# Left factors of w1, w2 loaded one factor at a time, two right factors in two buffers, and the next group's sums an item sooner

## The chip, the cores and the metric

One core of one Trainium2 chip runs the whole program. The metric is device time in microseconds (us), of one execution. Three executions of the kernel before took 1446.51, 1443.76 and 1447.54 us (median 1446.51). A fourth one, taken with the profiler, took 1452.29 us.

## The reference

```python
p_packed = sm_attn(p, k, v)             # 8 batches, 8 heads, 576 rows of 64, 32 packed rows
attn_out = sm_attn(q, p_packed, p_packed)
x = attn_out.transpose(0, 2, 1, 3).reshape(4608, 512)
h = x @ w_in                            # 512 x 2048
x2 = (h * (1 / (1 + exp(-h)))) @ w_out  # 2048 x 512
a, b = x2 @ w1, x2 @ w2                 # 512 x 1024 each
out = ((a * b) @ w3) @ w_out2           # 1024 x 1024, then 1024 x 512
```

All inputs and the output are float32. The kernel multiplies in a reduced form (float32r): each operand is split into a high part and the rest, and each product is made of three matmuls, high by high, rest by high, high by rest (`mm3`, lines 97 to 100; `split`, lines 82 to 91: ScalarE or VectorE makes the high part, VectorE or GpSimd subtracts it).

## The kernel before, in words

**Two stages.** The first stage makes x2, 256 items of 18 matmuls (`emit_h`, `emit_g`, `emit_x2`). Beside it run three streams of side work, paced by tables of (first item, last item, steps): stream "x" does the attention and later the weights w3 and w_out2, "y" the products of attention and w_in, and "z" (`decode_late`, line 914) decodes weights that the second stage needs. A "z" step is either one of 12 decodes that are only stored for later, or a step of one of four pairs of w1, w2 blocks; a pair takes two decodes and 11 steps that make and store seven left factors.

**The second stage** (from line 1117) makes a and b, their product, and the last product, by a Strassen-Winograd scheme: seven products of 2x2 blocks in place of eight. x2 is cut into 6 groups (g) of 768 rows. Each group has 4 items (mp), each a quarter of the inner width of a and b. An item has two halves, x = 0 for w1 and x = 1 for w2. In a half, `emit_ab` runs seven products (`product`, line 1306): a left factor of w1 or w2 (names a11, a12, a22, s1 to s4) by a right factor of x2 (b11, t1, b21, t2, t3, b22, t4, tiles `xcb` and `xct`), six matmuls of 384 columns each. ScalarE and VectorE take the results out of PSUM (tiles `p`, `u`, `y`); in the half x = 1 they also make the left factors of the last product (tiles `lfa`, `lfs`, sums in `tmp`). The last product of item i (`o_steps`, 63 matmuls of 256 columns, PSUM `ps_o`, running sums `o`) is put between the products of item i+1, with w34, the right factors made of w3 and w_out2, which `second_right_factors` makes in the first items.

**What the change touches.** Before, the left factors of a half come in one load of 1792 KB (`unit`, `load_unit`, line 1199) into one of three buffers, and a buffer is loaded again when its whole half is done. `load_x2` (line 1123) brings the x2 rows of a group into `x2r`, one buffer; it is called after item 2 of the group before. `right_sums` (line 1176) makes four sums on GpSimd (line 1151: tiles `xt`, `x2r`, `zz`, `zz`), and `right_factors` (line 1193) splits b11, t1 and the other five, from the beginning of item 3's half x = 1; `right_part` writes each into its only buffer, so that it must wait until the old group's last product with that factor is done. The table `paces["z"]` (line 1105) gives the "z" stream 27 steps over items 70 to 101, 26 over 128 to 165, and 12 decodes over 168 to 205.

**What sets the order.** The program is written in the order above, with generators that are called a step at a time (`side`, `step()` in `emit_ab`); a scheduler then places the instructions of each engine. Each engine works through its own list in order. All loads here are issued by SyncE (SP) in one queue, the stores of `out` too.

Of the kernel before, what the change touches and what calls it, by code (L numbers as in the profile page):

```python
# [9 lines left out]
F32 = mybir.dt.float32  # L10
# [13 lines left out]
def attention_swiglu_chain(  # L24
# [115 lines left out]
    wi_d = dram.tile([4, DM, 512], F32, name="wi_d")  # L140
    w12_d = dram.tile([128, KM2 // 2, 2, 2, 7, 2, 128], F32, name="w12_d")
    w34_d = [dram.tile([128, 512], F32, name=f"w34_d{i}") for i in range(KM2)]
# [765 lines left out]
    def decode_late():  # L908
# [7 lines left out]

        raws = []

        def load():

            raws.append(raw())
            with tc.issue_after(behind["mr"]):
                DMA.dma_start(out=raws[-1], in_=late_srcs[len(raws) - 1])

        load()
        yield
        zs = []
        for n in range(MID):
            if n + 1 < MID:
                load()  # L930
            with hold("sg"):
                z = Decode(raws[n], room(n)).z
            if n >= KM2:
# [5 lines left out]
            if n % 2:  # L939
                x, kt = divmod(n // 2, 2)  # L940
                sums = at.tile([128, 4, 256], F32, tag="wi", name="sums", bufs=WI)

                def part(j, src):
                    t = at.tile([128, 2, 2, 128], F32R, tag="z", name="w12s", bufs=NZ)
                    split(t[:, :, 0], t[:, :, 1], src.rearrange("p (j n) -> p j n", j=2), eng=G if j % 2 else V)
                    store(out=w12_d[:, 2:4, x, kt, j], in_=t, age=1)
# [39 lines left out]
    def prepare_second():  # L986

        attn.close()
        with tc.tile_pool(name="dec2", bufs=1, side="right") as dp:
# [16 lines left out]
            def combine(n):  # L1006
# [4 lines left out]
                def part(j, src):  # L1011
                    t = dp.tile([128, 2, 2, 128], F32R, tag="w12s", name="w12s", bufs=4)
                    split(t[:, :, 0], t[:, :, 1], src.rearrange("p (j n) -> p j n", j=2))
                    store(out=w12_d[:, 0:2, x, kt, j], in_=t, age=0)

# [88 lines left out]
    over(at0 + 2, at0 + 17, [Spread(B - 1, 0), Spread(B - 1, 1)])  # L1104
    paces["z"] += [(70, 101, 27), (128, 165, 26), (168, at0 + 13, MID - KM2)]
    prep_end = at0 + 2 * H2 - 6
# [12 lines left out]
    assert NG * GT == NT  # L1119
    x2r, x2c, w34 = {}, {}, {}  # L1120
    LEFT = {name: j for j, name in enumerate(("a11", "a12", "a22", "s1", "s2", "s3", "s4"))}

# [22 lines left out]
    def right_part(g, name, src, eng=None):  # L1145
        c = early.tile([128, 2, 2, W], F32R, tag=f"xc{name}", name=f"xc{name}")
        split(c[:, :, 0], c[:, :, 1], src, eng=eng)
        x2c[g][name] = c
# [30 lines left out]
    def right_sums(g):  # L1179
# [11 lines left out]
        yield  # L1191

    def right_factors(g):

        x2c[g] = {}
        for n, name in enumerate(RIGHT):
            right_part(g, name, sums_of[g][name], V if n % 2 else G)
            yield

    wunits, came2 = [], []  # L1200

    def load_unit():

        n = len(came2)
        mp, x = divmod(n % (2 * MP), 2)
        t = wunits[n % len(wunits)]
        behind["unit"] = move(out=t, in_=w12_d[:, mp, x]).ins
        came2.append(t)

    def room_unit(pool):  # L1210
        wunits.append(pool.tile([128, 2, 7, 2, 128], F32R, name=f"unit{len(wunits)}"))

# [40 lines left out]
    for i, (b, f, m) in enumerate(items):  # L1253
# [14 lines left out]
        if i == prep_end:  # L1268
# [4 lines left out]
            load_x2(0)  # L1273
            for _ in range(2):
                room_unit(early)
                load_unit()
            for mp in range(2):
                load_z34(mp)
            drain(first_right_factors())
# [18 lines left out]

    side = [second_right_factors()]
    next(side[0])  # L1300
    top = ctx.enter_context(tc.tile_pool(name="top", bufs=1))
    room_unit(top)
    load_unit()

    items2 = [(g, mp) for g in range(NG) for mp in range(MP)]

    def product(bank, w, g, left, right, first, last):

        xt = x2c[g][right]
        for kt in range(2):  # L1310
            for n, (wp, xp) in enumerate(((0, 0), (1, 0), (0, 1))):
                T.matmul(  # L1312
                    out=bank, lhsT=w[:, kt, LEFT[left], wp], rhs=xt[:, kt, xp],
                    start=first and (kt, n) == (0, 0), stop=last and (kt, n) == (1, 2),
                    skip_group_check=True,
                )

    ORDER = ("a11", "a22", "s1", "s2", "a12", "s4", "s3")
    lefts = {}

    def emit_ab(i):
# [18 lines left out]
        for x in range(2):  # L1340
            wt = came2[2 * i + x]
            nxt = side[0]
# [62 lines left out]
            step()  # L1405
            while len(came2) < min(2 * len(items2), 2 * i + x + 1 + len(wunits)):
                load_unit()
        while waiting:
# [140 lines left out]
```

## Time and profile before

| | |
|---|---|
| median of three runs | 1446.51 us (1443.76 to 1447.54) |
| profiled execution | 1452.29 us; span from first to last instruction 1450.2 us |
| TensorE (PE) busy | 1378.3 us, 95% of the span, 9188 matmuls |
| VectorE (DVE), GpSimd (POOL), ScalarE (ACT) busy | 1014.1, 900.2, 735.6 us |
| mean granted TensorE clock | 0.986 of full |

PE is the engine that sets the end: it is busy in nearly every stretch. A time can fall by PE's idle time, and by the stretches in which its clock is granted at half. The span runs from 0 to 1450 us; the second stage begins at about 870 us. Where a row says `[3.15 <-DVE y L1330]`, the engine was idle for 3.15 us before that instruction, and a VectorE instruction of line 1330 that writes tile y ended the wait.

### The profile page before, as it was taken

The numbers are of one execution on the slowest core, as the hardware profiler recorded it, in microseconds if no ns is written. First come the engines' busy times: TensorE is split into PE (matmuls) and PEld (weight loads), VectorE is DVE, ScalarE is ACT, GpSimd is POOL, SyncE is SP. The second block draws the span as 40 slices with busy tenths as digits, with TensorE's granted clock in tenths as the row PEclk, the third lists the DMA queues.
The fourth block names the chain that finished last, engine by engine and source line by source line (L and its number), as shares of the span: only waits on it lengthen the run. The fifth ranks groups of instructions, "written<-read, shape, count | busy, mean of one in ns | idle before, by whom it ended". The sixth has DMA issues, their size and how long they took to land.

```text
span 1450.2 us, 25891 instructions
## 1 busy us (share of the span) xinstructions
PE 1378.3 (95%) x9188; PEld 1322.4 (91%) x9188; DVE 1014.1 (70%) x1768; ACT 735.6 (51%) x1643; POOL 900.2 (62%) x854
## 2 busy tenths in 40 slices
PE   7799899999999999999999999999999899999998
PEld 5488799989999999999999998999999899899897
DVE  5897856568964589877678848685584756656756
ACT  6866556555665555665556645343334333333332
POOL 2768855756867666798677635374473644744733
PEclk9999999999999999999999999999999999999999
DMA  8598545745655445676647565455546545465541
GB/s 315 191 307 254 162 148 158 213 144 172 215 167 151 139 147 151 193 234 203 191 139 250 186 226 200 152 196 196 201 162 226 196 159 196 146 222 221 186 163 44
DMA packets 149922, 272.75 MB, mean 188 GB/s; under 512 B 14113, under 2 KB 107553, under 8 KB 143649
## 3 DMA queue, kind: packets, MB, share of 16 engines
q1 hardware_dynamic: 131680, 251.18, 52.5%
q10 hardware_dynamic: 18112, 19.93, 3.9%
q8 instruction: 72, 1.18, 0.3%
q14 instruction: 58, 0.47, 0.1%
HBM read 208.93 MB, written 62.13 MB: 187 GB/s over the span
## 4 chain that ended last, share of the span: by engine, by line
PE 65%; DVE 16%; ACT 5%; DMA 5%; issue 4%; POOL 2%; SPq 2%; POOLq 0%; ACTq 0%; DVEq 0%
PE ps_a L1312 11%; PE ps_o L1444 10%; PE ps_x L100 6%; PE ps_x L99 6%; PE ps_x L98 6%; PE ps_e L1312 6%; PE ps_h L98 3%; PE ps_h L100 3%; PE ps_h L99 3%; PE ps_b L1312 3%; DVE y L1330 2%; SPq L115 1%; DVE gg L846 1%; DMA mr<-m_d 1%; DMA x2r<-x_d 1%
## 5 line engine op out<-in xcount | busy, mean ns | idle before, releaser
L98 PE MATMUL ps_x<-gh,wo 128*128 128x288 f32 x1024 | 301.1, 297 | 2.0 <-ACT gh L82 1.2
L99 PE MATMUL ps_x<-gh,wo 128*128 128x288 f32 x1024 | 300.4, 296 | 0.0
L100 PE MATMUL ps_x<-gl,wo 128*128 128x288 f32 x1024 | 290.7, 297 | 3.3 <-POOL gl L91 3.2
L91 POOL TENSOR_TENSOR gl<-gg,gh 128x288 fp32r<-128x288 f32 x256 | 231.7, 908 | 98.7 <-ACT gh L82 79.9
L1426 DVE TENSOR_TENSOR o<-o,ps_o 128x768 f32<-128x768 f32 x144 | 136.3, 949 | 105.8 <-PE ps_o L1444 85.3
L91 POOL TENSOR_TENSOR mq<-mr,mq 128x256 fp32r<-128x256 f32 x168 | 140.4, 836 | 96.2 <-DVE mq L86 51.8
L98 PEld LDWEIGHTS ps_x<-gh,wo 128*128 128x128 f32 x1024 | 192.5, 188 | 4.9 <-ACT gh L82 1.4
L846 DVE SCALAR_TENSOR_TENSOR gg<-sg,ps_h 128x288 f32<-128x288 f32 x256 | 114.3, 447 | 116.1 <-ACT sg L841 59.3
L99 PEld LDWEIGHTS ps_x<-gh,wo 128*128 128x128 f32 x1024 | 192.7, 188 | 2.0 <-issue 1.2
L100 PEld LDWEIGHTS ps_x<-gl,wo 128*128 128x128 f32 x1024 | 188.4, 189 | 6.7 <-POOL gl L91 5.9
L82 ACT ACTIVATE gh<-gg 128x288 fp32r<-128x288 f32 x256 | 112.8, 443 | 155.8 <-DVE gg L846 147.8
L1312 PE MATMUL ps_a<-xct,unit 128*128 128x384 f32 x864 | 180.1, 342 | 6.2 <-DVE y L1330 5.5
L98 PE MATMUL ps_h<-a,mq 128*128 128x288 f32 x512 | 156.2, 305 | 19.2 <-DVE gg L846 14.9
L1312 PEld LDWEIGHTS ps_a<-xct,unit 128*128 128x128 f32 x864 | 150.8, 191 | 8.5 <-DVE y L1330 6.4
L99 PE MATMUL ps_h<-a,mq 128*128 128x288 f32 x512 | 152.5, 298 | 0.0
L100 PE MATMUL ps_h<-a,mq 128*128 128x288 f32 x512 | 152.1, 297 | 0.1
L841 ACT ACTIVATE sg<-ps_h 128x288 f32<-128x288 f32 x256 | 102.9, 404 | 64.7 <-PE ps_h L100 46.3
L91 POOL TENSOR_TENSOR lfa<-y,lfa 128x384 fp32r<-128x384 f32 x69 | 74.4, 1079 | 83.3 <-ACT lfa L82 83.1
L1444 PE MATMUL ps_o<-w,lfs 128*128 128x256 f32 x828 | 121.4, 283 | 4.2 <-DVE lfs L91 3.6
L98 PEld LDWEIGHTS ps_h<-a,mq 128*128 128x128 f32 x512 | 96.9, 189 | 28.5 <-DVE gg L846 21.4
L1444 PEld LDWEIGHTS ps_o<-w,lfs 128*128 128x128 f32 x828 | 113.6, 190 | 5.4 <-DVE lfs L91 4.4
L91 POOL TENSOR_TENSOR lfs<-tmp,lfs 128x384 fp32r<-128x384 f32 x69 | 78.4, 1144 | 39.7 <-ACT lfs L82 38.6
(198 smaller groups left out, 3211.7 us busy)
## 6 DMA issues: line engine op xcount, KB each, us to landing
unit<-w_d SPq DMA_DIRECT2D x48, 1792.0 KB, 6.9
mr<-m_d SPq DMA_DIRECT2D x144, 128.0 KB, 2.5
raw<-in_moe_w_dram SPq DMA_DIRECT2D x32, 512.0 KB, 4.4
w_d<-w12s ACTq DMA_DIRECT2D x56, 256.0 KB, 2.8
wz<-wi_d SPq DMA_DIRECT2D x48, 256.0 KB, 3.8
m_d<-ms SPq DMA_DIRECT2D x96, 128.0 KB, 3.0
x_d<-xs SPq DMA_DIRECT2D x20, 576.0 KB, 3.6
raw<-in_moe_w_out_dram SPq DMA_DIRECT2D x22, 512.0 KB, 4.4
```

What stands on the lines that cost most here:

```text
L82: A.activation(out=dst, in_=src, func=ACTF.Copy, scale=mul)
L91: (eng or V).tensor_tensor(out=lo, in0=src, in1=hi.bitcast(F32), op=ALU.subtract)
L98: T.matmul(out=dst, lhsT=wh, rhs=xh, start=start, stop=False)
L99: T.matmul(out=dst, lhsT=wl, rhs=xh, start=False, stop=False)
L100: return T.matmul(out=dst, lhsT=wh, rhs=xl, start=False, stop=stop)
L115: return eng.dma_start(out=out, in_=in_)
L841: ins = A.activation(out=sg, in_=ps, func=ACTF.Tanh, scale=0.5)
L846: ins = V.scalar_tensor_tensor(out=gg, in0=sg, scalar=1.0, in1=ps, op0=ALU.add, op1=ALU.mult)
L1312: T.matmul(out=bank, lhsT=w[:, kt, LEFT[left], wp], rhs=xt[:, kt, xp], start=first and (kt, n) == (0, 0), stop=last and (kt, n) == (1, 2), ...
L1330: eng.tensor_tensor(out=out, in0=in0, in1=in1, op=kind)
L1426: V.tensor_tensor(out=oacc[k], in0=oacc[k], in1=ps, op=ALU.add)
L1444: T.matmul(out=ps[:, t], lhsT=l[:, lp], rhs=w[:, wp], start=fresh and t != 1 and n == 0, stop=done and t != 0 and n == 2, skip_group_check ...
```

## The change

Four parts. (1) The left factors lie in DRAM by factor (`w12_d`), and each factor of a half is loaded alone (256 KB, `load_left`), into one of two buffers of its own; the load for two halves later is issued behind the factor's product. (2) b11 and t1 have a second buffer, used by the odd groups, in the room that the third unit had. (3) The next group's x2 rows are loaded after item 1 (in the first group after item 0); its sums and its b11 and t1 (now both split on GpSimd) are called from item 2 on, one in three steps; the other five are split in item 3's half x = 1 as before. In the first group `second_right_factors` is called with one step at a time where it had two in item 0, and the sums come right behind it. (4) The "z" stream has the 12 stored decodes in two lots of six between the pairs, and its table is 14 steps over items 70 to 101, 6 over 102 to 126, 26 over 128 to 165, 6 over 166 to 190, 13 over 191 to 206.

```diff
-    w12_d = dram.tile([128, KM2 // 2, 2, 2, 7, 2, 128], F32, name="w12_d")
+    w12_d = dram.tile([128, KM2 // 2, 2, 7, 2, 2, 128], F32, name="w12_d")
...
+        order_late = [0, 1, *others[:6], 2, 3, 4, 5, *others[6:], 6, 7]
...
-    paces["z"] += [(70, 101, 27), (128, 165, 26), (168, at0 + 13, MID - KM2)]
+    paces["z"] += [(70, 101, 14), (102, 126, 6), (128, 165, 26), (166, 190, 6), (191, at0 + 14, 13)]
...
+    TWICE = ("b11", "t1")
...
     def right_part(g, name, src, eng=None):
-        c = early.tile([128, 2, 2, W], F32R, tag=f"xc{name}", name=f"xc{name}")
+        pool = top[0] if g % 2 and name in TWICE else early
+        c = pool.tile([128, 2, 2, W], F32R, tag=f"xc{name}", name=f"xc{name}")
...
+    def two_right_factors(g):
+
+        x2c[g] = {}
+        for name in TWICE:
+            right_part(g, name, sums_of[g][name], G)
+            yield
+
     def right_factors(g):
 
-        x2c[g] = {}
         for n, name in enumerate(RIGHT):
-            right_part(g, name, sums_of[g][name], V if n % 2 else G)
+            if name not in TWICE:
+                right_part(g, name, sums_of[g][name], V if n % 2 else G)
             yield
 
-    def load_unit():
...
+    def group_sums(g):
+        for gen in (right_sums(g), two_right_factors(g)):
+            for _ in gen:
+                yield
+                yield
+                yield
+
+    def load_left(n, name):
+
+        if n < 2 * len(items2):
+            mp, x = divmod(n % (2 * MP), 2)
+            t = early.tile([128, 2, 2, 128], F32R, tag=f"w{name}", name=f"w{name}", bufs=2)
+            behind["unit"] = move(out=t, in_=w12_d[:, mp, x, LEFT[name]]).ins
+            came2[n, name] = t
...
+    def first_group():
+        yield from second_right_factors()
+        yield from right_sums(1)
+        yield from two_right_factors(1)
...
+        w = came2.pop((n2, left))
...
-                    out=bank, lhsT=w[:, kt, LEFT[left], wp], rhs=xt[:, kt, xp],
+                    out=bank, lhsT=w[:, kt, wp], rhs=xt[:, kt, xp],
...
+        load_left(n2 + 2, left)
...
-                for _ in range(1 if i else 2):
-                    next(nxt, None)
+                next(nxt, None)
...
-        if mp == MP - 1 and g + 1 < NG:
+        if g and mp == 2 and g + 1 < NG:
             drain(side[0])
-            side[0] = right_sums(g + 1)
+            side[0] = group_sums(g + 1)
         emit_ab(i)
-        if mp == MP - 2 and g + 1 < NG:
+        if mp == (1 if g else 0) and g + 1 < NG:
             load_x2(g + 1)
```

**POOL's list from the last item of group 2 towards group 3.** Of the kernel before (`tmp`, `lfa`, `lfs` are an item's own left factors, the rest is the next group's right side):

```order
L91 TENSOR_TENSOR lfa_14641<-y_14532,lfa_14641 128x384
L1151 TENSOR_TENSOR xt<-x2r 128x768
L91 TENSOR_TENSOR xcb_14798<-x2r,xcb_14798 128x2x384
L91 TENSOR_TENSOR xcb_14774<-x2r,xcb_14774 128x2x384
L1151 TENSOR_TENSOR x2r<-x2r 128x2x384
L1151 TENSOR_TENSOR zz<-x2r,xt 128x768
L91 TENSOR_TENSOR lfa_14795<-y_14764,lfa_14795 128x384
L91 TENSOR_TENSOR xct_14840<-x2r,xct_14840 128x2x384
L1151 TENSOR_TENSOR zz<-x2r,zz 128x768
L1330 TENSOR_TENSOR tmp<-y_14764,y_14766 128x384
```

Of the changed kernel, one item sooner, and then the beginning of what is left for the last item:

```order
L91 TENSOR_TENSOR lfs_14692<-tmp,lfs_14692 128x384
L91 TENSOR_TENSOR xcb_14941<-x2r,xcb_14941 128x2x384
L1159 TENSOR_TENSOR xt<-x2r 128x768
L1159 TENSOR_TENSOR x2r<-x2r 128x2x384
L1159 TENSOR_TENSOR zz<-x2r,xt 128x768
L91 TENSOR_TENSOR xct_14995<-xt,xct_14995 128x2x384
L91 TENSOR_TENSOR lfa_14867<-y_14836,lfa_14867 128x384
L1159 TENSOR_TENSOR zz<-x2r,zz 128x768
```

```order
L91 TENSOR_TENSOR xcb_15125<-x2r,xcb_15125 128x2x384
L91 TENSOR_TENSOR lfa_15122<-y_15091,lfa_15122 128x384
L91 TENSOR_TENSOR xct_15171<-x2r,xct_15171 128x2x384
L1351 TENSOR_TENSOR tmp<-y_15091,y_15093 128x384
```

The four sums, b11 and t1 stand a whole item ahead, with one left factor of item 2 among them; in the last item POOL has three of the next group's instructions (b21, t3, later t4).

**DVE's list in items 0 and 1**, where w34 is made (`w34sums` and `zz` are its sums, `w` its splits). Before, between two of item 0's adds that read `ps_a`:

```order
L1330 TENSOR_TENSOR y_12120<-p_12117,ps_a 128x384
L977 TENSOR_TENSOR w34sums<-zz,w34sums 128x256 x3
L91 TENSOR_TENSOR w_0_12104<-w34sums,w_0_12104 128x256 x2
L91 TENSOR_TENSOR w_1_12102<-w34sums,w_1_12102 128x256 x2
L91 TENSOR_TENSOR w_0_12104<-w34sums,w_0_12104 128x256
L1330 TENSOR_TENSOR y_12205<-p_12202,ps_a 128x384
```

And now:

```order
L1351 TENSOR_TENSOR y_12142<-p_12139,ps_a 128x384
L91 TENSOR_TENSOR w_0_12128<-w34sums,w_0_12128 128x256
L980 TENSOR_TENSOR w34sums<-zz,w34sums 128x256
L91 TENSOR_TENSOR w_1_12126<-w34sums,w_1_12126 128x256 x2
L91 TENSOR_TENSOR w_0_12128<-w34sums,w_0_12128 128x256
L91 TENSOR_TENSOR w_1_12126<-w34sums,w_1_12126 128x256
L91 TENSOR_TENSOR w_0_12128<-w34sums,w_0_12128 128x256
L1351 TENSOR_TENSOR y_12225<-p_12222,ps_a 128x384
```

Eight instructions for w34 stood between the two adds, and seven stand there now.

**SP's list around the x2 load for group 3** (with the semaphores that each waits for, the landings of earlier loads in turn among eight of them). Before:

```order
L115 DMA unit_12111<-w_d 128x3584 [waits DMAHW7_49,DMAHW3_49,PE_49]
L115 DMA unit_11869<-w_d 128x3584 [waits DMAHW5_49,PE_49]
L115 DMA x2r<-x_d_0_91 128x4x288 [waits DMAHW1_49,Activation_49,Pool_49]
L115 DMA x2r<-x_d_1_92 128x4x288 [waits DMAHW2_49]
L115 DMA x2r<-x_d_0_93 128x4x192
```

And now:

```order
L115 DMA ws_14767<-w_d 128x512 [waits DMAHW4_49,PE_49]
L115 DMA wa_14688<-w_d 128x512 [waits DMAHW5_49,PE_49]
L115 DMA x2r<-x_d_0_91 128x4x288 [waits DMAHW6_49,Pool_49]
L115 DMA x2r<-x_d_1_92 128x4x288 [waits DMAHW7_49]
L115 DMA x2r<-x_d_0_93 128x4x192 [waits DMAHW0_49]
L115 DMA ws_14788<-w_d 128x512 [waits DMAHW1_49,PE_49]
```

The x2 load has two loads of 256 KB right ahead of it in the place of two of 1792 KB; every load waits for the landing of the one eight places ahead.

**ACT's list in the first group's item 1:**

```order
L82 ACTIVATE p_12473<-ps_a 128x384
L82 ACTIVATE lfs_12321<-tmp 128x384
L82 ACTIVATE xcb_12996<-x2r 128x2x384
L82 ACTIVATE w_3_12713<-zz 128x256
L82 ACTIVATE o_12413<-ps_o 128x768
L82 ACTIVATE p_12474<-ps_e 128x384
```

The high part of group 1's b11 (`xcb_12996`) stands ahead of two instructions that take results out of PSUM for PE, and it reads x2 rows that are loaded after item 0.

## Rows read from the trace of the kernel before

**Rows 1.** The page: each engine's busy us, share of the span, instructions.
```profile
PE 1378.3 (95%) x9188; PEld 1322.4 (91%) x9188; DVE 1014.1 (70%) x1768; ACT 735.6 (51%) x1643; POOL 900.2 (62%) x854
```

**Rows 2.** By stretch: length, busy PE, PEld, DVE, ACT, POOL, clock, DMA share, GB/s.
```profile
288.00:395.00 107.00, 100.51 (x734) 97.72 (x732) 83.97 (x190) 61.17 (x154) 71.61 (x75) 0.98 0.56 171
471.00:600.00 129.00, 124.69 (x937) 122.80 (x936) 102.88 (x228) 73.18 (x183) 89.42 (x96) 1.00 0.51 153
600.00:712.00 112.00, 110.48 (x789) 106.97 (x788) 79.00 (x140) 66.15 (x148) 88.55 (x87) 1.00 0.65 203
870.00:912.00 42.00, 36.34 (x195) 34.69 (x196) 35.28 (x55) 22.89 (x58) 23.43 (x23) 0.92 0.45 175
912.00:1441.00 529.00, 511.67 (x3324) 505.77 (x3323) 341.31 (x449) 193.14 (x372) 279.94 (x223) 0.99 0.50 180
```

**Rows 3.** PE's waits in order of time, 889 to 910 us: start, length, instruction, idle before.
```profile
891.59 0.66 PE L1312 MATMUL ps_a<-xct,unit 128*128 128x384 f32 x2 [1.95 <-DVE y L1330]
909.36 1.01 PE L1312 MATMUL ps_a<-xct,unit 128*128 128x384 f32 x2 [3.15 <-DVE y L1330]
```

**Rows 4.** The same where group 1, 2, 3 and 4 begin.
```profile
969.08 0.97 PE L1312 MATMUL ps_e<-xct,unit 128*128 128x384 f32 x4 [1.74 <-DVE xct L91]
1062.49 0.85 PE L1312 MATMUL ps_e<-xct,unit 128*128 128x384 f32 x2 [1.98 <-DVE xct L91]
1158.98 1.33 PE L1312 MATMUL ps_b<-xcb,unit 128*128 128x384 f32 x3 [3.48 <-DVE y L1330]
1253.05 1.16 PE L1312 MATMUL ps_b<-xcb,unit 128*128 128x384 f32 x5 [1.13 <-DVE y L1330]
1259.80 1.41 PE L1444 MATMUL ps_o<-w,lfs 128*128 128x256 f32 x8 [2.47 <-DVE lfs L91]
```

**Rows 5.** The same where group 5 begins.
```profile
1346.46 0.74 PE L1444 MATMUL ps_o<-w,lfa 128*128 128x256 f32 x4 [1.19 <-DVE o L1426]
1352.77 1.21 PE L1444 MATMUL ps_o<-w,lfs 128*128 128x256 f32 x8 [1.12 <-DVE lfs L91]
```

**Rows 6.** PE alone by stretch: length, busy, clock; the second at full clock.
```profile
892.02:895.43 3.41, 3.41 (x13) 0.50 0.92 357
1000.00:1003.41 3.41, 3.41 (x22) 1.00 0.27 94
1062.69:1066.10 3.41, 3.41 (x12) 0.50 0.95 408
1158.26:1165.09 6.83, 6.11 (x20) 0.50 0.39 168
1260.66:1264.07 3.41, 3.41 (x14) 0.50 0.00 0
```

**Rows 7.** DVE in order of time, ahead of the wait of 3.48 us.
```profile
1154.57 1.82 DVE L1330 TENSOR_TENSOR y<-y,y 128x384 f32<-128x384 f32 x1
```

**Rows 8.** POOL in order of time at that place, and where x2 lands.
```profile
1142.06 1.85 POOL L1151 TENSOR_TENSOR xt<-x2r 128x768 f32<-128x768 f32 x1 [4.99 <-DMA x2r<-x_d]
1155.92 2.12 POOL L1151 TENSOR_TENSOR zz<-x2r,zz 128x768 f32<-128x768 f32 x1
```

**Rows 9.** DVE's instructions on tile y, 912 to 1441 us: count, ns min/median/max.
```profile
L1330 DVE TENSOR_TENSOR y<-y,y x68: 550/558/2196, 913.8 to 1431.8; 128x384 f32<-128x384 f32 x68
L1330 DVE TENSOR_TENSOR y<-p,ps_a x45: 539/554/556, 916.9 to 1431.3; 128x384 f32<-128x384 f32 x45
```

**Rows 10.** SP's waits, 870 to 1441 us: in total, times, longest.
```profile
SPq L115 <- PE ps_a L1312: 333.5, 34, 18.2
```

**Rows 11.** DMA issues, 870 to 1441 us: count, KB each, median us to landing.
```profile
unit<-w_d SPq DMA_DIRECT2D x45, 1792.0 KB, 6.8
x2r<-x_d SPq DMA_DIRECT2D x10, 576.0 KB, 9.2
zz<-w_d SPq DMA_DIRECT2D x4, 256.0 KB, 5.9
```

**Rows 12.** SP in order of time: one unit load's issue.
```profile
1130.69 0.32 SPq L115 DMA_DIRECT2D unit<-w_d  x1
```

More of the change, by code (lines that the diff above doesn't have):

```diff
@@ L917, in decode_late @@
         raws = []
+        others = list(range(KM2, MID))
+        order_late = [0, 1, *others[:6], 2, 3, 4, 5, *others[6:], 6, 7]
+        to_come = list(order_late)
         def load():
@@ L922, in load @@
             with tc.issue_after(behind["mr"]):
-                DMA.dma_start(out=raws[-1], in_=late_srcs[len(raws) - 1])
+                DMA.dma_start(out=raws[-1], in_=late_srcs[to_come.pop(0)])
         load()
@@ L927, in decode_late @@
         zs = []
-        for n in range(MID):
-            if n + 1 < MID:
+        for n in order_late:
+            if to_come:
                 load()
             with hold("sg"):
-                z = Decode(raws[n], room(n)).z
+                z = Decode(raws.pop(0), room(n)).z
             if n >= KM2:
@@ L945, in part @@
                     split(t[:, :, 0], t[:, :, 1], src.rearrange("p (j n) -> p j n", j=2), eng=G if j % 2 else V)
-                    store(out=w12_d[:, 2:4, x, kt, j], in_=t, age=1)
+                    store(out=w12_d[:, 2:4, x, j, kt], in_=t, age=1)
                 for step in left_factors(zs, sums, part):
@@ L1013, in part @@
                     split(t[:, :, 0], t[:, :, 1], src.rearrange("p (j n) -> p j n", j=2))
-                    store(out=w12_d[:, 0:2, x, kt, j], in_=t, age=0)
+                    store(out=w12_d[:, 0:2, x, j, kt], in_=t, age=0)
                 later.extend(left_factors(z, sums, part))
@@ L1120, in attention_swiglu_chain @@
     x2r, x2c, w34 = {}, {}, {}
+    USED = ("a11", "s1", "a12", "s2", "s3", "s4", "a22")
+    items2 = [(g, mp) for g in range(NG) for mp in range(MP)]
+    TWICE = ("b11", "t1")
+    top = []
     LEFT = {name: j for j, name in enumerate(("a11", "a12", "a22", "s1", "s2", "s3", "s4"))}
@@ L1191, in right_sums @@
         yield
+    def two_right_factors(g):
[3 more added lines that the diff above has]
+            yield
     def right_factors(g):
-        x2c[g] = {}
         for n, name in enumerate(RIGHT):
-            right_part(g, name, sums_of[g][name], V if n % 2 else G)
+            if name not in TWICE:
+                right_part(g, name, sums_of[g][name], V if n % 2 else G)
             yield
-    wunits, came2 = [], []
-    def load_unit():
[L1204 to L1211, printed above, removed]
+    def group_sums(g):
[4 more added lines that the diff above has]
+                yield
+    came2 = {}
+    def load_left(n, name):
[4 more added lines that the diff above has]
+            came2[n, name] = t
     z34 = {}
@@ L1273, in attention_swiglu_chain @@
             load_x2(0)
[L1274 to L1278, printed above, removed]
+            for n in range(2):
+                for name in USED:
+                    load_left(n, name)
+                load_z34(n)
             drain(first_right_factors())
@@ L1297, in room, with product @@
         return pool.tile(shape, dtype, tag=tag, name=tag)
-    side = [second_right_factors()]
-    next(side[0])
[L1301 to L1307, printed above, removed]
+    def first_group():
+        yield from second_right_factors()
+        yield from right_sums(1)
+        yield from two_right_factors(1)
+    side = [first_group()]
+    next(side[0])
+    top.append(ctx.enter_context(tc.tile_pool(name="top", bufs=1)))
+    def product(bank, n2, g, left, right, first, last):
         xt = x2c[g][right]
+        w = came2.pop((n2, left))
         for kt in range(2):
@@ L1340, in emit_ab @@
         for x in range(2):
-            wt = came2[2 * i + x]
+            wt = 2 * i + x
             nxt = side[0]
@@ L1405, in emit_ab @@
             step()
-            while len(came2) < min(2 * len(items2), 2 * i + x + 1 + len(wunits)):
-                load_unit()
         while waiting:
```

## The prediction, made before the changed kernel ran

> **What bounds the kernel now.** I read the page's busy times, then the busy times by stretch, then PE's waits in order of time, then the other engines just ahead of those waits. PE is busy 1378.3 us, 95% of the span [rows 1], so no change of order can give more than the other 5%, some 72 us, and what PE loses at half clock. The stretches show where that time lies [rows 2]. In 912 to 1441 us PE is idle for 529.00 - 511.67 = 17.3 us, in 870 to 912 for 42.00 - 36.34 = 5.7 us; that is the second stage. In the first stage, where the "z" table is changed, it is idle for 6.5 us (288 to 395), 4.3 us (471 to 600) and 1.5 us (600 to 712).
>
> In the second stage most of the idle time is a few waits. Two are in items 0 and 1, of 1.95 and 3.15 us, both ended by an add of DVE that takes a result out of PSUM [rows 3]. The others come once per group, at its beginning: 1.74 us for group 1, 1.98 for group 2, 3.48 for group 3, 1.13 and 2.47 for group 4 [rows 4], 1.19 and 1.12 for group 5 [rows 5]. The reader is to see that PE never waits for `unit`, the left factors: the waits end with DVE. Ahead of the longest one DVE spends 1.82 us on one `y<-y,y` [rows 7], whose median is 558 ns [rows 9], while POOL runs a sum of 2.12 us [rows 8]. POOL is late there because x2 landed late: it had waited 4.99 us for `x2r` [rows 8].
>
> Behind the long waits stands a second loss, the clock. Stretches of 3.41 us at half clock follow the waits of 1.95, 1.98, 3.48 (two of them, 6.83 us) and 2.47 us, and none follows 1.74 or the shorter ones [rows 3 to 6]. At half clock PE ran 13 matmuls in 3.41 us, at full clock 22 [rows 6]: a stretch costs 3.41 x 9 / 22 = 1.4 us. The mean clock of 0.92 over 42 us [rows 2] says that 870 to 912 holds two of them (8% of 42 us is 3.4 us of full clock, and each lacks half of 3.41).
>
> **The change part by part.** Sums are against the profiled execution, 1452.3 us with what lies around its span; the median of the three runs, 1446.5, is 5.8 us lower, and I subtract the same sum from it.
>
> (1) Loads by factor. 48 loads of 1792 KB become 336 of 256 KB with the same bytes. SP spends 0.32 us on an issue [rows 12], so 288 more take 288 x 0.32 = 92 us of SP in some 570 us; SP now spends 333.5 us waiting for PE to free units [rows 10], which covers it. If that cover were gone, loads would go out late, the second rival. Each factor has two buffers: its load is issued when its product is done and is needed two halves later. A half is 571 us / 48 = 11.9 us, so there are 23.8 us for it, and 256 KB landed in 5.9 us [rows 11]. Cost 0.
>
> Seven small loads for a large one is what a rule speaks against. The rows have 5.9 us to landing for 256 KB and 6.8 us for 1792 KB [rows 11], so most of it does not grow with size. The Trainium skill (DMA: Bandwidth & Descriptors, section Bandwidth) asks for transfers of 1 MiB or more, and its section on the anatomy of one DMA has a fixed 2 us in each; by its formula a factor is an estimated 2.6 us and a unit 6.1. Paid seven times in line that would be an estimated 18.2 us, over a half's length; paid side by side it changes nothing. No run here shows seven such loads under way.
>
> (2) and (3) Group begins 2 to 5. Removed from the last item: the four sums (about 2 us each on POOL, as the one of 2.12 [rows 8]), b11 and t1, and their wait for the old group's last products. POOL's list keeps three of the next group's instructions there, where it had eight. Moved to: item 2's first half, where DVE mostly reads PSUM. Its adds from PSUM take 539 to 556 ns whatever POOL does, while `y<-y,y` reaches 2196 [rows 9]; so the sums slow DVE less there. What is late next: DVE still splits t2 and b22 in the last item, ahead of the adds that free PSUM. I leave one wait of 1.2 us per begin, like the short ones of today [rows 5], and no half clock, since none followed waits of that size. Waits now 1.98 + 3.48 + 1.13 + 2.47 + 1.19 + 1.12 = 11.4 us, half clock 4 x 1.4 = 5.6 us, together 17.0; left 4.8; gain 12.2 us. Bounds: all of it, 17.0, and 0.
>
> Group 1's begin: 1.74 [rows 4] to 1.2, gain 0.5 us; bounds 1.7 and 0.
>
> Items 0 and 1. Though w34 is called at half the rate, DVE's list still has seven of its instructions between two adds where it had eight. So I take an eighth of 1.95 + 3.15, 0.6 us. The gain could be all, 5.1 + 2 x 1.4 = 7.9 us. It could be a loss: ACT now has the split of group 1's b11 in item 1, ahead of two instructions that empty PSUM for PE, and it waits there for x2 rows; POOL's 4.99 us [rows 8] is the price at that end.
>
> (4) The "z" table. In 288 to 395 us there are 27 "z" steps now and 14 then. PE's loss there is 6.5 us of waits and a half-clock stretch (mean clock 0.98 [rows 2]), 1.4 us; I take half, 4 us, as gain. The 13 steps removed turn up at 666 to 704 us, where the old table had 5 of its 12 decodes, beside the attention of the last batch; I charge 2 us, near the 1.5 that this stretch loses [rows 2]. Net 2 us, bounds 8 gain (all of it) and 6 loss (what moves costs there what it cost before, 6.5).
>
> Sum: 0 + 12.2 + 0.5 + 0.6 + 2 = 15.3 us. 1452.3 - 15.3 = 1437 for a profiled run, **1431 us** for the median.
>
> **The rivals.** *The bunch only moves (no difference).* POOL's list now has five of the next group's instructions in a row, a sixth behind one left factor of item 2, together about 12 us, and they begin only when x2 has landed. If it lands 9.2 us after its issue [rows 11], the block ends some 21 us into an item of 23.8 us, and item 2's left factors, which follow on POOL, come late for the products of item 3. For it: POOL waited 4.99 us for x2 before, and DVE's instructions with two SBUF inputs slow down wherever POOL runs [rows 7, 9]. The Trainium skill (SBUF — State Buffer, section Who interferes with whom) has it that those contend with GpSimd's reads and those with one SBUF input do not; the trace agrees, 2196 against 556 ns. Against it: the loads ahead of x2 are 256 KB now, so that it should land sooner. Price: a wait of 2 us and a half-clock stretch, 3.4 us, in five groups, 17 us: what (2) and (3) gave goes back, and 1446 to 1448 us is the time.
>
> *Loads become the bound (slower).* SP's list shows each load waiting for the landing of the one eight places ahead, so at most eight are under way. A group has 56 factor loads, 3 or 4 of x2 and 4 stores: 64 in turn on eight semaphores, 8 landings one after the other in about 95 us (group begins at 969, 1062, 1159 [rows 4]). This decides as soon as a landing takes over 95 / 8 = 11.9 us. Rows of before have 5.9, 6.8 and 9.2 us [rows 11]; against it also that the DMA engines are busy half the time, 0.50 [rows 2]. At 12.5 us a group takes 100 us: 6 x 5 = 30 us lost, 15 gained, 1461 us. The rule of the Trainium skill on small transfers, above, would do it in this way.
>
> **How the numbers follow.** The forecast with its bounds has a chance of 0.75, the moved bunch 0.16, the loads 0.09. The best end is 17.0 + 1.7 + 7.9 + 8 = 34.6 us, 1412 us. The worst end of the forecast has (2) and (3) at half, 6, a loss of 5 in items 0 and 1, and 6 in the first stage: 5 us slower than now. That all three go wrong together is unlikely, and the moved bunch ends near 1447, so the range is 1412 to 1447 us. About 0.3% (4.3 us) is what a measurement can tell from no change. Faster 0.75, within it 0.16, slower 0.09.
>
> **What would show it.** Right: group begins with waits of some 1.2 us or less and a granted clock of 1.00 there; the rows of `xt` on POOL beginning in item 2, not in the last item; PE waiting nowhere for a `w` factor's DMA; the two waits in items 0 and 1 still there. Wrong: PE waits ended by POOL `lfa` or `lfs` about an item before a group begins (the moved bunch); PE waits ended by a DMA of `wa` or `ws`, or SP rows with landings over 12 us (the loads); ACT waiting for `x2r` in item 1 with PE behind it; new waits of PE at 660 to 710 us.

## The result and the profile after

| | before | after |
|---|---|---|
| median of four runs each, us | 1447.03 (1443.76 to 1448.73) | 1425.7 (1424.89 to 1427.32) |
| profiled execution, its span, us | 1452.29, 1450.2 | 1427.32, 1425.5 |
| start of the second stage, us | 870.0 | 864.4 |

The ratio is 0.9857, interval 0.9837 to 0.9876: 20.7 us less by the ratio (the medians differ by 21.3). The forecast was 1431, range 1412 to 1447.

The page and the stretches of after, to be laid beside [rows 1, 2]; the last two begin 6 us earlier, as the second stage does, and end 9 us ahead of the span's end, as there. The page first:

```profile
PE 1368.4 (96%) x9188; PEld 1315.7 (92%) x9188; DVE 1016.3 (71%) x1763; ACT 733.5 (51%) x1643; POOL 903.0 (63%) x859
```

Then the stretches, with their columns:

```profile
288.00:395.00 107.00, 104.44 (x776) 102.71 (x776) 81.44 (x192) 61.35 (x152) 70.38 (x79) 0.98 0.55 168
600.00:712.00 112.00, 111.73 (x807) 109.42 (x807) 84.19 (x143) 67.92 (x155) 86.52 (x89) 1.00 0.61 190
864.00:906.00 42.00, 35.43 (x207) 33.41 (x208) 35.96 (x57) 23.41 (x58) 25.58 (x24) 1.00 0.76 244
906.00:1416.00 510.00, 502.26 (x3318) 499.29 (x3318) 337.38 (x445) 190.51 (x372) 283.23 (x228) 1.00 0.60 182
```

The second stage after items 0 and 1, up to 9 us ahead of the end, lost 19 us of length (529 to 510). PE's idle time there fell from 17.3 to 7.7 us, and the clock column from 0.99 to 1.00. In 864 to 906, items 0 and 1, PE is idle for 6.6 us where it was 5.7: nothing was gained there but the clock (0.92 to 1.00). 288 to 395 went from 6.5 to 2.6 us idle, and 600 to 712 from 1.5 to 0.3.

The best single measure of the group begins is the stretch from the start of group 1 to the start of group 5, which holds the same products in both kernels. Busy times by stretch, of before:

```profile
963.60:1341.70 378.10, 365.68 (x2364) 362.11 (x2363) 243.84 (x318) 140.19 (x269) 204.94 (x161) 0.98 0.52 190
```

The same of after:

```profile
957.50:1317.00 359.50, 356.65 (x2364) 355.62 (x2363) 238.17 (x314) 138.91 (x270) 209.74 (x165) 1.00 0.65 199
```

It is 18.6 us shorter. (A second trace of the old second stage, that of the version with the new "z" table alone, has 377.4 us here.) PE's idle time in it (length less busy time) is 12.4 us before and 2.9 after. Of the 9.0 us that PE is busy for less, some 5.6 are the four half-clock stretches of [rows 6] that lie in it, at the estimate of 1.4 us each; the other 3.4 us this view doesn't resolve. Group 0 is 0.5 us shorter and the last group, with the end, as long as before within 0.1 us. So of the 24.7 us of span, 5.6 come from the first stage, 0.5 from group 0 and 18.6 from groups 1 to 4. The profiled execution of before lies 5.3 us above its median, that of after 1.6 us above its own, so some 4 of the 24.7 us belong to these two executions; the part on the "z" table shows that the first stage is where such a difference can lie.

These are the waits of PE that are left in groups 0 to 5 and last over 0.9 us, ahead of the end (waits in order of time, to be laid beside [rows 3 to 5]):

```profile
883.58 1.32 PE L1332 MATMUL ps_a<-xct,wa 128*128 128x384 f32 x6 [2.42 <-DVE y L1351]
898.59 1.33 PE L1462 MATMUL ps_o<-w,lfs 128*128 128x256 f32 x9 [1.43 <-DVE lfs L91]
919.35 1.31 PE L1462 MATMUL ps_o<-w,lfs 128*128 128x256 f32 x9 [1.52 <-ACT lfs L82]
1119.59 0.62 PE L1462 MATMUL ps_o<-w,lfa 128*128 128x256 f32 x3 [1.40 <-DVE o L1444]
```

None stands where a group begins, and none ends with a DMA. Landings, in the view of DMA issues (count, KB each, median us to landing), beside [rows 11]:

```profile
ws<-w_d SPq DMA_DIRECT2D x184, 256.0 KB, 3.0
wa<-w_d SPq DMA_DIRECT2D x138, 256.0 KB, 3.1
x2r<-x_d SPq DMA_DIRECT2D x10, 576.0 KB, 6.5
```

The 256 KB loads land in a median of 3.0 to 3.1 us. By their issues and landings in the trace mostly two or three of them were under way at once, and never more than six. Paid in line, seven would be 21 us, longer than a half, and the time shows none of that. The Trainium skill's formula (DMA: Bandwidth & Descriptors, Anatomy of one DMA — SWDGE (gpsimd) path), from which the prediction had an estimated 2.6 us for each, was fitted to transfers that GpSimd issues; these are issued by SyncE, and the measured 3.0 us decides.

### The profile page after: what moved, and what is told of

Its sections match the earlier page's. It is cut to its first block, busy times and chain, and to the rows that moved or that the text cites. A ratio compares the mean times of both kernels' runs of the same rounds, so it can differ in the third digit from the quotient of the medians.

```text
span 1425.5 us, 26714 instructions
## 1 busy us (share of the span) xinstructions
PE 1368.4 (96%) x9188; PEld 1315.7 (92%) x9188; DVE 1016.3 (71%) x1763; ACT 733.5 (51%) x1643; POOL 903.0 (63%) x859
## 4 chain that ended last, share of the span: by engine, by line
PE 68%; DVE 15%; issue 5%; DMA 4%; ACT 4%; POOL 3%; SPq 1%; POOLq 0%; ACTq 0%; DVEq 0%
PE ps_a L1332 12%; PE ps_o L1462 12%; PE ps_x L100 6%; PE ps_x L99 6%; PE ps_e L1332 6%; PE ps_x L98 6%; PE ps_h L98 3%; PE ps_h L100 3%; PE ps_h L99 3%; PE ps_b L1332 3%; DVE y L1351 2%; DVE gg L846 2%; DMA m_d<-ms 1%; DVE x L91 1%; DVE mq L86 1%
## 5 line engine op out<-in xcount | busy, mean ns | idle before, releaser
L91 POOL TENSOR_TENSOR gl<-gg,gh 128x288 fp32r<-128x288 f32 x256 | 228.8, 896 | 99.8 <-ACT gh L82 82.7
L98 PEld LDWEIGHTS ps_h<-a,mq 128*128 128x128 f32 x512 | 96.9, 189 | 26.3 <-DVE gg L846 19.1
L1332 PE MATMUL ps_a<-xct,ws 128*128 128x384 f32 x576 | 117.8, 336 | 0.0
L1332 PEld LDWEIGHTS ps_a<-xct,ws 128*128 128x128 f32 x576 | 99.8, 188 | 0.4 <-ACT p L82 0.3
L99 PEld LDWEIGHTS ps_h<-a,mq 128*128 128x128 f32 x512 | 97.0, 190 | 2.7 <-issue 1.0
```

The lines of the kernel that those rows point to most:

```text
L91: (eng or V).tensor_tensor(out=lo, in0=src, in1=hi.bitcast(F32), op=ALU.subtract)
L98: T.matmul(out=dst, lhsT=wh, rhs=xh, start=start, stop=False)
L99: T.matmul(out=dst, lhsT=wl, rhs=xh, start=False, stop=False)
L1332: T.matmul(out=bank, lhsT=w[:, kt, wp], rhs=xt[:, kt, xp], start=first and (kt, n) == (0, 0), stop=last and (kt, n) == (1, 2), skip_group_ ...
```

## The experiments

Each ratio is to runs of the kernel before on the same chip. "Idle" is PE's idle time from the start of group 1 to the start of group 5 (by version, up to nine output matmuls of 0.12 us more or less than in before fall into it), "ahead" the time by which the first sum `xt` starts on POOL ahead of its group (groups 1 to 5), both from that version's trace.

| version | median us | ratio | interval | idle us | ahead us |
|---|---|---|---|---|---|
| before (trace of before) | 1447.03 | 1 | | 12.4 | 2 to 7 |
| after | 1425.7 | 0.9857 | 0.9837 to 0.9876 | 2.9 | 29 to 53 |
| loads by factor alone | 1447.31 | 0.9999 | 0.9985 to 1.0012 | 10.6 | 6 to 11 |
| after, single buffers | 1424.01 | 0.9847 | 0.9832 to 0.9861 | 1.3 | 30 to 54 |
| after, x2 late | 1438.59 | 0.9942 | 0.9927 to 0.9957 | 11.3 | 5 to 9 |
| after, sums only called late | 1425.34 | 0.9847 | 0.9831 to 0.9864 | 2.4 | 29 to 53 |
| after, sums held to the last item | 1430.39 | 0.9879 | 0.9863 to 0.9895 | 3.0 | 16 to 22 |
| after, sums held to the last half | 1444.49 | 0.9974 | 0.9963 to 0.9984 | 14.3 | 3 to 7 |
| before, x2 early | 1428.31 | 0.9868 | 0.9853 to 0.9883 | 1.1 | 27 to 51 |

**Part (1) alone**: loads by factor, the rest as before.

```diff
+        w = came2.pop((n2, left))
...
-                    out=bank, lhsT=w[:, kt, LEFT[left], wp], rhs=xt[:, kt, xp],
+                    out=bank, lhsT=w[:, kt, wp], rhs=xt[:, kt, xp],
...
+        load_left(n2 + 2, left)
```

> The kernel before with part (1) alone: loads by factor, everything else as it was. Theory A (the four sums taken out of the last item bring most of the gain at the group begins): no gain there, 1444 to 1449 us, the begins still wait 1 to 3.5 us. Theory C (x2 was late because two loads of 1792 KB stood ahead of it): x2 lands 2 to 4 us sooner, POOL's wait of 4.99 us goes, and 4 to 8 us are gained: 1439 to 1443 us. If loads of 256 KB cost anything, PE waits for w factors show it, above 1449 us.

It neither costs nor gains time: 336 loads for 48 are free here, as forecast. Its stretch from group 1 to group 5:

```profile
957.30:1328.50 371.20, 360.56 (x2354) 356.78 (x2353) 245.99 (x317) 138.22 (x270) 204.72 (x160) 0.99 0.64 193
```

x2 did land sooner, as theory C foretold (8 to 9 us from the first of its issues to the last landing, where before has 11 to 12), and the sums start 6 to 11 us ahead. But POOL still waits for x2 (who waited for whom, 940 to 1330 us; in total, times, longest), and the begins keep most of their idle time:

```profile
POOL xt L1153 <- DMA x2r<-x_d: 13.8, 4, 3.8
```

The stretch is 6.9 us shorter than before's in this one trace, and the last group, 114.6 us for 108.5, takes nearly all of that back; no gain is left in the time.

**The second buffers away.** The other parts as in the change; all seven splits of the right factors in the last half.

```diff
-        pool = top[0] if g % 2 and name in TWICE else early
+        pool = early
...
-        for gen in (right_sums(g), two_right_factors(g)):
+        for gen in (right_sums(g),):
```

> The changed kernel without the second buffers: x2 and the sums early, all seven splits in the last item's half x = 1. Theory A: the begins lose little, 1425 to 1430 us. Theory B (b11 and t1, which no longer wait for the old group's last products, bring the gain): waits of PE for xcb and xct splits come back, 2 us and more each, with half clock behind some: 1433 to 1441 us.

As fast as the change: doubling b11 and t1 brings nothing that can be measured.

**x2 late, and x2 early with the sums called late.** Both keep the doubled factors and call the sums in the last item; the first also loads x2 after item 2, as before.

```diff
-        if g and mp == 2 and g + 1 < NG:
+        if mp == MP - 1 and g + 1 < NG:
             drain(side[0])
             side[0] = group_sums(g + 1)
...
-        if mp == (1 if g else 0) and g + 1 < NG:
+        if mp == MP - 2 and g + 1 < NG:
             load_x2(g + 1)
```

> The changed kernel with the second buffers, but x2 loaded after item 2 and the sums called in item 3, as before. Theory A: POOL has its sums and DVE its slow instructions in the last item again, 10 to 14 us come back: 1435 to 1440 us. Theory B: 1425 to 1430 us.

> As the run before, but x2 loaded early (after item 1) and only the sums called in item 3. Theory C: with x2 there in time nothing is late, 1425 to 1430 us. Theory A: as the run with both late, 1435 to 1440 us, unless the scheduler itself moves the sums ahead, which the time of the first sum on POOL would show.

The late load gives back 0.0085 to 0.0095 of the time, 12 to 14 us. The other one loses nothing, but it did not do what its edit says: the first sum starts at 905.3 us, in the change at 905.0. The tile scheduler puts the sums where x2 lets them start, whatever the item that calls them. So this version tells only that calling them sooner is not needed.

**The sums held.** To keep them late with x2 early, they have to stand behind an instruction on POOL: once behind its last difference of the item before, once behind its split of a11 in the last half of the group (the last part of the diff; the part ahead of it is the first version's). In the second the other five splits are called later too, three steps at a time.

```diff
         for gen in (right_sums(g), two_right_factors(g)):
-            for _ in gen:
+            for _ in range(4 if gen.__name__ == "right_sums" else 2):
+                with hold("late"):
+                    next(gen)
                 yield
...
-            eng.tensor_tensor(out=out, in0=in0, in1=in1, op=kind)
+            ins = eng.tensor_tensor(out=out, in0=in0, in1=in1, op=kind)
+            if eng is G:
+                behind["late"] = ins.ins
...
+            ins = split(c[:, 0], c[:, 1], a[name], eng=eng)
+            if eng is G:
+                behind["late"] = ins.ins
```

> The changed kernel, x2 loaded early as there, but the four sums and the two splits on POOL stand behind POOL's last difference of the item before the last, so that none of them can start before the last item of a group. The version in which the sums were merely called in the last item had its first sum at 905.3 us, as the changed kernel at 905.0, so it did not hold them back, and its 1425 us tells nothing of where the sums should stand. Theory A (it is the sums in the last item that make PE wait, since they hold up DVE and the splits there): about 1438 us, as the version with the late load of x2 (1438.6), with waits of 1 to 2 us again at the group begins. Theory C (what matters is that x2 has landed when the last item starts; POOL has room for the sums there): 1425 to 1429 us.

> The changed kernel with x2 loaded early, the four sums and the two splits on POOL held behind POOL's split of a11 in the last half of a group, so that they begin some 6 to 8 us ahead of the next group, as in the version with the late load, though x2 has landed long before. In the version held to the start of the last item they began 17 to 22 us ahead and its group begins lost nothing. Theory L (what counts is how long ahead of the group the sums start; the load only gates them): the begins lose again what the version with the late load lost, 1436 to 1440 us. Rival C2 (the late load itself is what hurts, as by ACT waiting for x2 in front of its copies out of PSUM, 20.9 us in that version): 1425 to 1430 us.

Held to the last item, the first sum of group 3 on POOL (order of time), for a group that begins at 1134.6 us:

```profile
1118.10 2.16 POOL L1159 TENSOR_TENSOR xt<-x2r 128x768 f32<-128x768 f32 x1
```

The same version from the start of group 1 to the start of group 5 (busy times by stretch):

```profile
956.10:1315.00 358.90, 355.87 (x2354) 354.36 (x2353) 235.25 (x313) 140.03 (x268) 204.80 (x162) 1.00 0.64 200
```

Held to the last half, the same sum, for a group that begins at 1142.4:

```profile
1137.37 1.85 POOL L1159 TENSOR_TENSOR xt<-x2r 128x768 f32<-128x768 f32 x1
```

And this version's stretch, then (PE's waits in order of time) its longest wait, at the begin of group 2:

```profile
955.10:1331.50 376.40, 362.06 (x2354) 358.41 (x2353) 239.94 (x312) 138.47 (x267) 210.04 (x164) 0.99 0.63 190
```
```profile
1055.07 1.33 PE L1471 MATMUL ps_o<-w,lfa 128*128 128x256 f32 x9 [3.71 <-DVE o L1453]
```

Held to the start of the last item, 16 to 22 us ahead, the sums do no harm at the begins: 358.9 us, with nine output matmuls (about 1 us) fewer in it, against 359.5 in the change. At group 5, which begins where this stretch ends, the longest wait near the begin is 1.00 us. So the last item is not the wrong place in itself, and theory A falls for the begins. Yet the version takes 1430.39 us, just above theory C's range and 5 us more than the one only called late. Most of that lies outside this stretch (in the traces the last group takes 113.8 us here and 108.7 there); what takes it wasn't tried apart.

Held to 3 to 7 us ahead, with x2 landed 27 us and more before the sums, the begins lose nearly all again: 376.4 us, and a wait of 3.71 us ended by DVE. So the loss does not need a late load, which speaks for theory L; 1444.49 us is more than either theory had foretold. Against the version only called late it loses 18 us by the ratios, where the late load lost 14. That its other five splits too are called later may be why; how much is the sums' and how much the splits' wasn't tried apart. ACT's waits for x2, of which C2 thought, hardly tell the versions apart. Who waited for whom, from the start of group 1 to that of group 5 (us in total, times, longest), of the change, where the begins lose little, and then of the version with the late load:

```profile
ACT xcb L82 <- DMA x2r<-x_d: 14.6, 4, 5.6
ACT xcb L82 <- DMA x2r<-x_d: 17.5, 4, 5.2
```

**One line.** The kernel before with the load of x2 moved, nothing else.

```diff
-        if mp == MP - 2 and g + 1 < NG:
+        if mp == (1 if g else 0) and g + 1 < NG:
             load_x2(g + 1)
```

> The kernel before with one line changed: the next group's x2 is loaded after item 1 of a group (after item 0 in group 0) as in the changed kernel, no longer after item 2. The loads by unit, single buffers, the calls of the four sums in the last item and the "z" table stay as they were. Theory C (x2 is there too late for POOL's sums, and that is all that is wrong at the group begins): PE's losses at the begins of groups 1 to 5 go as in the changed kernel, so 1447 - 17 = 1430 us, and no wait over 1.5 us stands there. Theory A (the sums have to be called an item sooner, or the loads by factor and the doubled right factors are needed for it): 1440 us or more.

Its stretch from group 1 to group 5:

```profile
958.10:1317.50 359.40, 358.32 (x2371) 357.00 (x2371) 241.50 (x320) 137.97 (x269) 198.08 (x161) 1.00 0.56 199
```

POOL at the first sum of group 3, which begins at 1139.8 (order of time):

```profile
1111.73 1.85 POOL L1151 TENSOR_TENSOR xt<-x2r 128x768 f32<-128x768 f32 x1 [6.51 <-DMA x2r<-x_d]
```

It gives 19.1 us (0.0132 of 1447). POOL still waits for x2, by 6.51 us here, longer than the 4.99 of [rows 8]; but 28 us ahead of the group that wait costs nothing.

**The "z" table** with its order of the weights, put alone into before, and taken out of the change.

```diff
+        order_late = [0, 1, *others[:6], 2, 3, 4, 5, *others[6:], 6, 7]
...
-    paces["z"] += [(70, 101, 27), (128, 165, 26), (168, at0 + 13, MID - KM2)]
+    paces["z"] += [(70, 101, 14), (102, 126, 6), (128, 165, 26), (166, 190, 6), (191, at0 + 14, 13)]
```

> The kernel before with the new "z" table and the new order of the late factors, nothing else. In the profiles of before and of the change the second stage begins 5.6 us earlier (869.5 and 863.9 us), and up to there the change touches nothing but this table. Theory R (the table gives those 5.6 us): about 1441 us against 1447, the second stage beginning near 864 us, and the long waits at the group begins all still there. Rival S (the 5.6 us come from what the tile scheduler does with the whole program, since loads of the second stage are issued during the first; or they scatter from run to run): within 2 us of the kernel before. My forecast charged 2 us for what moves to the end of the stage: by that, a gain of 2 us, 1445.

> The changed kernel with the old "z" table and the old order of the late factors. Theory R: it loses the 5.6 us of the first stage and keeps the second, so 1431 us, with the second stage beginning near 870 us and taking the same time as in the changed kernel. Rival S: 1426 us as the changed kernel.

Alone it gives 3.9 us (ratio 0.9973, 0.9963 to 0.9982), less than theory R's 6 and more than rival S's 2. Without it the change takes 1429.36 us (0.9872, 0.9855 to 0.9889), 2.2 us more by the ratios, with intervals that overlap. The stretch from item 70 to the last item, where the table works (busy times by stretch), of before with the new table:

```profile
292.60:866.40 573.80, 564.62 (x3999) 546.68 (x3997) 430.94 (x844) 335.31 (x784) 401.00 (x415) 0.99 0.58 183
```

Of the change with the old one:

```profile
289.50:865.10 575.60, 564.06 (x4010) 545.24 (x4008) 425.19 (x844) 334.69 (x784) 404.63 (x415) 1.00 0.58 182
```

In ten profiles of versions with the new table it lasts 573.0 to 574.1 us; in four with the old one 579.0 (before), 577.2, 575.6 and 575.8. So the table is worth 2 to 4 us, and the 5.6 us between the two profiles have some chance in them.

**Items 0 and 1.** Once two steps of w34 per call in item 0 as before, once each step held on DVE behind the latest add out of PSUM.

```diff
-                next(nxt, None)
+                for _ in range(1 if i else 2):
+                    next(nxt, None)
```
```diff
             for step in right_steps(z, sums, part):
-                step()
+                with hold("ab") if "ab" in behind else ExitStack():
+                    step()
```

> The changed kernel with two steps of the decode of w34 called per step in item 0, as in the kernel before. My forecast gave the halved rate 0.6 us. Theory F (the tile scheduler fills DVE's list there by what is ready, whatever the rate of the calls): 1425 to 1427 us, with the same waits of PE in items 0 and 1. Rival H (the halved rate is what took the two half-clock stretches away): 1428 to 1430 us, with half-clock stretches between 885 and 912 us.

> The changed kernel with each step of the decode of w34 held on DVE behind the latest add that takes a product out of PSUM, so that DVE's list in items 0 and 1 has at most a few other instructions between two of those adds. The changed kernel has 5.9 us of waits of PE there, ended by adds of DVE and by DVE's splits. Theory D (DVE's list bunches, seven instructions between two adds, and that is what PE waits for): the waits of items 0 and 1 go, 1420 to 1422 us. Rival E (DVE has too much work there whatever its order; or the held steps are then late for the first outputs, which wait for w34): the waits stay or come later, 1426 us or more.

The first took 1426.51 us (0.9850, 0.9837 to 0.9864): the halved rate does nothing that the time shows. Its group 0 has the wait of the change and this time half clock behind it, as rival H foretold, but not the time that H foretold. The half clock does not hang on the rate either: with the sums held to the last item, at the rate of the change, group 0 has two such stretches too. The second took 1424.04 us (0.9832, 0.9814 to 0.9850), between the two forecasts, and its group 0 is 91.3 us where the change has 93.1. The wait of 2.42 us is gone, but one of 2.56 stands later, ended by a split of DVE, so theory D holds for one of the two only, and the gain of 2 us is inside the intervals.

**Three small edits to the kernel before**: the early load, the new order and table of "z", and the held steps.

```diff
-        if mp == MP - 2 and g + 1 < NG:
+        if mp == (1 if g else 0) and g + 1 < NG:
...
+        order_late = [0, 1, *others[:6], 2, 3, 4, 5, *others[6:], 6, 7]
...
+    paces["z"] += [(70, 101, 14), (102, 126, 6), (128, 165, 26), (166, 190, 6), (191, at0 + 14, 13)]
...
+                with hold("ab") if "ab" in behind else ExitStack():
+                    step()
```

> The kernel before with three small edits: x2 loaded after item 1, the new "z" table, and the decode of w34 held step by step behind DVE's adds. It keeps the loads by unit and single buffers. Theory C: each edit gives what it gave alone, 17 at the group begins, 2 to 4 in the first stage, 2 to 3 in items 0 and 1, so 1447 - 22 = 1425 us, as fast as the changed kernel or faster. Theory A: 1435 us or more, as the group begins keep their waits.

1425.27 us, ratio 0.9831 (0.9814 to 0.9848): it does what the whole change does, without loads by factor, second buffers or earlier calls. Its interval overlaps with that of the change, so I call neither the faster.

## Why the prediction was right, and where not

The time and the direction held; the reason given for the largest term did not. That the number came near is in part luck: the change also loads x2 an item sooner, which the prediction did not price, and that alone brings what it gave to other parts.

- **(1), 0 us**: right. Part (1) alone is 0.9999, and PE waits for no `w`.
- **(2) and (3), 12.2 us, and group 1, 0.5**: measured 18.6 us in groups 1 to 4, for which the prediction's own terms come to 10.8 - 4.8 + 5.6 = 11.6 us (waits, what is left of them, half clock). The size was low: I left 4.8 us there, and 2.9 of idle time are left; the 3.4 us of busy time weren't in my sum. At group 5 the waits of [rows 5] went, but the last group is no shorter; 6.83 us at half clock now stand near its end (granted clock 0.97, before 1.00), which may be why.
- **What brings it**. The step that failed is "Removed from the last item: the four sums, b11 and t1, and their wait": I gave the gain to what is taken out of the last item. The runs show that second buffers bring nothing that can be measured, that the place of the calls brings nothing, and that at the begins the sums do no harm in the last item if they start at its beginning. The load of x2 moved alone brings 19.1 us. What counts at the begins is that the chain x2, sums, splits starts early enough: 16 us ahead of the group was enough, 3 to 11 were not, and the old load allowed 2 to 7. I had the row in hand ("POOL is late there because x2 landed late") and made it a remark, not a term.

How a late start becomes a wait is argued, not shown, from 20 us about the begin of group 3 (busy times by stretch, the same columns: PE, PEld, DVE, ACT, POOL). Before:

```profile
1144.00:1164.00 20.00, 16.04 (x85) 15.20 (x84) 19.15 (x18) 7.37 (x13) 18.81 (x11) 0.86 0.38 150
```

Sums held to the last half, then to the last item:

```profile
1138.00:1158.00 20.00, 16.98 (x106) 16.01 (x105) 16.87 (x18) 8.64 (x15) 20.00 (x13) 1.00 0.53 150
1130.00:1150.00 20.00, 18.63 (x121) 17.99 (x120) 17.27 (x20) 8.48 (x16) 20.00 (x13) 1.00 0.55 169
```

After:

```profile
1132.00:1152.00 20.00, 19.36 (x129) 19.04 (x128) 16.83 (x22) 8.11 (x16) 14.46 (x11) 1.00 0.55 171
```

Before, POOL is busy for 18.8 of the 20 us, and DVE for 19.2 with 18 instructions, 1.06 us each; after, POOL has 5.5 us free and DVE does 22 in 16.8 us, 0.77 each. With the sums held to the last half POOL has no free time, and DVE again does 18, 0.94 each. The slowing can be seen on one instruction, the difference `tmp<-y,y`, which DVE does in before just ahead of the add that empties ps_b and ends the wait of 3.48 us, beside POOL's sum of 2.12 us [rows 4, 8]. DVE in before, in order of time:

```profile
1156.42 2.04 DVE L1330 TENSOR_TENSOR tmp<-y,y 128x384 f32<-128x384 f32 x1
1158.39 0.54 DVE L1330 TENSOR_TENSOR y<-p,ps_b 128x384 f32<-128x384 f32 x1
```

DVE in after, at the same place of the program:

```profile
1141.11 0.55 DVE L1351 TENSOR_TENSOR tmp<-y,y 128x384 f32<-128x384 f32 x1
1141.58 0.54 DVE L1351 TENSOR_TENSOR y<-p,ps_b 128x384 f32<-128x384 f32 x1
```

So DVE's being slowed was rightly seen, and that it ends because the sums have been done by then, whatever their item, fits the runs. But POOL's free time alone is not the reason: with the sums held to the last item POOL is busy for all of the 20 us, and PE is idle for 1.4 us only; in after POOL is at work beside the `tmp<-y,y` of 0.55 us too, on a split of 1.38 us; and at group 4 DVE needs 0.94 us each before and 0.87 after, a small difference. Two of the waits of [rows 4], 1.74 and 1.98 us, were ended by a split of the chain itself. How the loss divides between late splits and slowed instructions stays open.

- **Items 0 and 1, 0.6 us**: 0.5 us for group 0, which is near by luck, and waits stayed, as foretold. The reason, the halved rate, is not one. PE's idle time in group 0 rose from 5.7 to 7.7 us, and half-clock stretches went (clock 0.96 to 1.00). Group 0 in before, then in after:

```profile
870.00:963.60 93.60, 87.94 (x540) 86.29 (x541) 67.11 (x99) 41.31 (x92) 46.69 (x43) 0.96 0.52 194
864.40:957.50 93.10, 85.42 (x540) 82.95 (x541) 72.88 (x101) 41.96 (x94) 54.02 (x46) 1.00 0.62 193
```

- **(4), 2 us net**: near, 2 to 4 us by the runs. The charge of 2 us at 666 to 704 did not come: 600 to 712 is idle 0.3 us, less than before.
- **The rivals**: the moved bunch did not come, since the sums start 29 us or more ahead and no wait of PE over 1.5 us stands from the start of group 1 to that of group 5. The loads did not: 3.0 us is far from the 11.9 at which they decide. The Trainium skill (SBUF — State Buffer, Who interferes with whom) still agrees with DVE's rows in after: `y<-y,y` up to 2177 ns, `y<-p,ps_a` never above 556.

## What to carry to other kernels

Where PE waits for DVE at a stage's begin, follow the chain back past the engine named to the load that starts it, and try first to issue that load sooner: here one line gave what the whole rewrite gave, within the intervals. And look in the trace whether an edit moved the work at all: under a scheduler that orders by what is ready, a call in another place may change nothing; here, with x2 loaded early, only an explicit order held the sums late.

## What was not expected of the hardware

A long wait of PE is not always followed by half clock. The wait in item 0 is the same in the change and in the version with two steps per call (2.42 and 2.43 us, the same instruction), yet the 3.41 us after it were at full clock in the first and at half in the second. PE by stretch, of after:

```profile
883.60:887.01 3.41, 3.41 (x22) 1.00 1.02 335
```

The same of the version with two steps:

```profile
882.26:885.67 3.41, 3.41 (x13) 0.50 0.95 330
```

So the bound that I read off [rows 3 to 6], half clock after 1.95 us and more, is no rule: the same wait was followed by half clock in one trace and not in another.

Nor is the price of a half-clock stretch always lost. PE in order of time behind that wait, of after (the wait's own row stands above):

```profile
886.85 1.21 PE L1332 MATMUL ps_a<-xcb,wa 128*128 128x384 f32 x6
892.61 1.31 PE L1332 MATMUL ps_b<-xcb,wa 128*128 128x384 f32 x6 [0.72 <-DVE y L1351]
```

Of the version with two steps, from the wait on:

```profile
881.92 2.03 PE L1332 MATMUL ps_a<-xct,wa 128*128 128x384 f32 x6 [2.43 <-DVE y L1351]
886.75 1.21 PE L1332 MATMUL ps_a<-xcb,wa 128*128 128x384 f32 x6
890.94 1.33 PE L1332 MATMUL ps_b<-xcb,wa 128*128 128x384 f32 x6
```

The product `ps_a<-xcb` begins 3.27 us behind the end of the wait at full clock and 4.83 us at half, so this stretch cost 1.56 us. But `ps_b<-xcb` begins 9.03 and 9.02 us behind it: at full clock PE had to wait for DVE twice more, for 0.41 us and for the 0.72 us of the row, and at half clock it did not. So the estimate of 1.4 us is near what such a stretch costs, but here it was lost only until PE's next waits.
